# A state-space convolution with a gated FFN: tables loaded by pieces, negated sines made on chip, tensors given in the tiles' order, raw rows turned earlier

## The chip, the cores and the metric

The kernel runs on one core of a Trainium2 chip. The metric is the device time of one execution in microseconds (us), as a median over runs. The engines are TensorE (PE, matmuls), VectorE (DVE), ScalarE (ACT), GpSimd (POOL) and SyncE (SP, which here only issues DMAs). Each engine works through its own queue in order; engines wait for each other by semaphores. ACT and POOL can issue DMAs too.

## The reference

```python
x = A_u                                   # 1 x 2048 x 512
xn = layernorm(x)
K  = real(sum_n C[d,n] * exp(dt*A[d,n] * l) * dt*B[d,n])      # d: 512, l: 2048, n: 128
s  = irfft(rfft(xn, 4096) * rfft(K, 4096))[:2048] + xn * Dskip # causal convolution per channel
g  = silu(gelu(xn @ w1 + b1) @ w2 + b2)                        # 512 -> 1792 -> 512
return x + s * g
```

## The kernel before, in words

The first two thirds of the time go to the feed-forward part g (four tiles of 512 tokens, twice, once for each half of the hidden units) and, woven into it by the hand-written `ORDER` (L48), to the convolution kernel K. Both leave their results in DRAM: `gd` (the gate g, L186) and `kgd` (K, L190), and the normalized rows in `xs`. The time studied here is what follows.

**The seam** (L1037 to L1063). The last feed-forward pieces (`S`, `L`: `second_part`, dense matmuls of 128x512; `A`: silu on ACT) run between the first transforms of block 0 (`F00`, `F01`, `F10`, `F11`: `first_dft` on PE, L848, and `first_out`, L859, which copies its four PSUM banks to the tile X, two on ACT and two on DVE). Ahead of that loop stand, in the program: `z_load`, the load of the table `mc` in four pieces (`table_load`, L790), `side_skip(0)` on POOL (L843: adds the skip weight to block 0's kernel rows `in<-kgd`), `side_turn(1)` on ACT (L822: turns the 128x1024 halves of block 1's raw rows from `raw` into `in`), `kernel_load(1)` and `side_skip(1)`. Behind the loop come `z_store` (L438: the last tile of g goes to `gd`; four stores issued by POOL), then the loads of the tables `tcn` (four pieces) and `gc`. The tiles that the blocks use are opened over space that `zi`, the tile of g, has held.

**The blocks** (L1064). A Fourier transform of length 4096 is done as two transforms, 32 by 64. The 512 channels are four blocks of 128, each of eight slots (`slot(b, g)`, L966). A slot issues, in this order of the program:

- PE: the second transform `s` of four of the 32 frequencies (`second_dft`, L866, 64 matmuls of 64x64 against `mc`, which holds cosines, sines and negated sines); in some slots `sa`, the first inverse transform (`back_dft`, L904, against `tcn`); in slot 5 `y`, the last inverse transform of the block before (`last_dft`); in even slots the first transform of the next block.
- ACT: a copy `uh` of half of `s` (`spectrum`, L879), the copies Z out of `sa` (`back_out`, L914), the copies X out of the first transform.
- DVE: the products of both halves (`product`, L888), which free the PSUM tile of `s`, of which there are two; in slot 5 `last_out` (L954: four products of `y` with the gate `gb`, and on POOL four adds of x); in odd slots `combine` (L894: two adds into Y, which `sa` reads); the 32x32 transposes (`turn`).
- DMAs at the end of the slot: the gate and x for the block's output (`tail_load`, L932: in each of slots 0 to 3 two loads of `gb` and four of `xb`; x is read from the input in 512-byte rows), the raw rows two blocks ahead (`side_piece`, in slots 3 to 6), the output of the block before (`store`, L962, slot 7, 512-byte rows). In slot 7 ACT then turns the raw rows two blocks ahead (`side_turn`), both halves at once.

`bank` (L800) hands out the PSUM banks for the first transform, `sa` and `y` in turn, from two pools of two banks each; a first transform and a `y` take four, a `sa` two. A bank is free again when its copies or products have read it.

**The end** (L1067 to L1088). The last block's inverse transforms run split in halves: `sa` in two parts, transposes, `y` in two parts, then products and adds on DVE and POOL, and the store in eight DMAs, four on SP's queue and four on ACT's.

Of the kernel before, what the change touches and what calls it, by code (L numbers as in the profile page):

```python
# [11 lines left out]
F32 = mybir.dt.float32  # L12
# [8 lines left out]
P = 128  # L21
# [4 lines left out]
N1, N2 = 32, 64  # L26
NB = 4
# [103 lines left out]
def _shape_constants():  # L131
    n1 = np.arange(N1)[:, None]
    k1 = np.arange(N1)[None, :]
    a = 2 * np.pi * n1 * (k1 + 0.25) / N1
    cf = np.tile(np.stack([np.cos(a), -np.sin(a)], 1), (G, 1, 1))
    cg = np.stack([np.cos(a).T, -np.sin(a).T], 1).reshape(2, 2, 4, 2, 2, N1)
    cg = np.tile(cg.transpose(1, 3, 2, 4, 0, 5).reshape(1, N1, 2, N1), (G, 1, 1, 1))
    n2 = np.arange(N2)[:, None]
    k2 = np.arange(N2)[None, :]
    cm = np.zeros((2, N2, N1, 3, N2))  # L140
    ct = np.zeros((2, N2, N1, 2, N2))
    for k in range(N1):
        th = 2 * np.pi * (n2 * (k + 0.25) / L + n2 * k2 / N2)
        c, s = np.cos(th), np.sin(th)
        cm[:, :, k, 0, :] = c
        cm[:, :, k, 1, :] = s
        cm[:, :, k, 2, :] = -s
# [11 lines left out]
    return {  # L159
        "cf": cf.reshape(P, 2 * N1).astype(f),  # L160
        "cg": cg.reshape(P, 2 * N1).astype(f),
        "cm": cm.reshape(P, N1 * 3 * N2).astype(f),
        "ct": ct.reshape(P, N1 * P).astype(f),
        "cb": cb.reshape(CH * NPC, CH * NPH).astype(ml_dtypes.bfloat16),
    }
# [3 lines left out]
def kernel(  # L169
    ctx: ExitStack, tc: tile.TileContext,  # L170
    u, a_re, a_im, b_re, b_im, c_re, c_im, log_dt, dskip, w1, b1, w2, b2,
    cf, cg, cm, ct, cb, out,
# [3 lines left out]

    x_t = u[0].rearrange("(n w q) d -> w n q d", n=N1, w=4)
    o_t = out[0].rearrange("(n w q) d -> w n q d", n=N1, w=4)
    x_l = u[0].rearrange("(r j q) d -> j r q d", j=2, q=NQ)
# [3 lines left out]
    xs_l = xs.rearrange("(r j q) d -> j r q d", j=2, q=NQ)  # L183
    xt_h = [dram.tile([KD, P, TB * P], F32R, name=f"xt_h{t}") for t in range(NTB)]
# [124 lines left out]
    def ln_load(n):  # L309
        if n == 2:  # L310
            ln["zi"] = wka.tile([P, TB, D], F32, tag="zi", name="x23")
        if n in (2, 3):
            x = ln["zi"][:, 2 * n - 4:2 * n - 2, :]
        else:
            x = wka.tile([P, 2, D], F32, tag="x", name=f"x{n}", bufs=2)
        for j in range(2):
            SY.dma_start(x[j * 64:(j + 1) * 64], x_l[j, :, 2 * n:2 * n + 2, :])
        ln[n] = x
# [31 lines left out]
    def ln_store(n):  # L350
        for j in range(2):
            SY.dma_start(xs_l[j, :, 2 * n:2 * n + 2, :], ln[n][j * 64:(j + 1) * 64])

# [435 lines left out]

    def table_load(t, src):  # L790
        w = t.shape[2] if len(t.shape) == 3 else t.shape[2] * t.shape[3]
        for k in range(0, N1, 8):
            d = t[:, k:k + 8]
            SY.dma_start(d.rearrange("p k m -> p (k m)") if len(t.shape) == 3 else d.rearrange("p k a m -> p (k a m)"),
                         src[:, k * w:(k + 8) * w])

# [24 lines left out]

    def side_turn(b):  # L822
        if b:
            t = SB["pf"].tile([P, DB, N2], F32, tag="in", name=f"in0_{b}", bufs=2)
        else:
            t = wka.tile([P, DB, N2], F32, tag="xl", name="in0_0", bufs=2)
        raw = side[b].rearrange("p m d -> p d m")
        side[b] = [[t[:, :DB // 2], t[:, DB // 2:]]]
        for h in range(2):
            d, r = side[b][0][h], raw[:, h * DB // 2:(h + 1) * DB // 2]  # L830
            A.copy(d, r)

# [33 lines left out]
    def second_dft(b, g):  # L866
        mc = SB["mc"]
        p = SB["ps"].tile([P, 2, 2, 2, 2, N2], F32, tag="ri", name=f"s2_{b}_{g}", bufs=2)
        for jj in range(2):
            for o in range(2):  # L870
                for c in range(2):
                    for ka in range(2):
                        for r in range(2):
                            k, h = 4 * g + 2 * jj + ka, slice(r * 64, (r + 1) * 64)
                            PE.matmul(p[ka * 64:(ka + 1) * 64, r, o, :, jj], mc[h, k, ((0, 2), (1, 0))[c][o], :],  # L875
                                      xf[b][h, c, :, k, :], start=(c == 0), stop=(c == 1), skip_group_check=True)
        sp[b, g] = p
# [54 lines left out]
    def tail_load(b, t):  # L932
        if b not in gx:
            gx[b] = new_tail(b)
        gt, xt_ = gx[b]
        q = slice(t * TB, (t + 1) * TB)
        gv = gd[b][t].rearrange("(j n h) (q m) -> h j n q m", j=2, h=2, m=P)
        for h in range(2):
            SY.dma_start(gt[64 * h:64 * h + 64, q], gv[h])
            for w in (2 * h, 2 * h + 1):  # L940
                SY.dma_start(xt_[w * N1:(w + 1) * N1, q], x_t[w, :, q, b * P:(b + 1) * P])  # L941

# [11 lines left out]
    def last_out(b, py):  # L954
        gt, xt_ = gx[b]
        for g in range(G):
            cs = slice(g * N1, (g + 1) * N1)
            gv = gt[:, :, cs]
            V.tensor_mul(gv, py[g].rearrange("p (q i) -> p q i", i=N1), gv)
            GP.tensor_add(xt_[:, :, cs], gv, xt_[:, :, cs])  # L960

    def store(b, q=slice(0, NQ), qs=(SY, SY, SY, SY)):  # L962
        for w in range(4):
            qs[w].dma_start(o_t[w, :, q, b * P:(b + 1) * P], gx[b][1][w * N1:(w + 1) * N1, q])

    def slot(b, g):  # L966
# [49 lines left out]
        if last and 2 < g < 7:  # L1016
            tail_load(b, g - 3)
        if b + 2 < NB and 2 < g < 7:
            if g == 3:
                side[b + 2] = SB["pf"].tile([P, N2, DB], F32, tag="in", name=f"raw{b + 2}", bufs=2)  # L1020
            side_piece(b + 2, g - 3)
        if b and g == 7:
            store(b - 1)
        if b + 2 < NB and g == 7:
            side_turn(b + 2)
            kernel_load(b + 2)
# [66 lines left out]
_INS = ["A_u", "A_A_re", "A_A_im", "A_B_re", "A_B_im", "A_C_re", "A_C_im", "A_log_dt", "A_Dskip",  # L1093
        "B_w1", "B_b1", "B_w2", "B_b2"]
_OUTS = [((1, L, D), "float32")]

# [22 lines left out]
```

## Time and profile before

| | |
|---|---|
| runs shown | 574.71, 575.71, 577.72 us; median 575.71 |
| the profiled execution | 574.02 us |
| its span, first to last instruction | 572.2 us |
| mean granted TensorE clock | 0.974 |
| PE busy | 538.6 us, 94% of the span |
| DVE busy | 453.2 us, 79% |
| ACT busy | 402.8 us, 70% |
| POOL busy | 280.8 us, 49% |
| DMA | 86.92 MB, 109706 packets, 43606 of them under 512 B |

Lines of the timeline read: start in us, duration in us, engine, source line, operation, tile written <- tiles read, shapes, count of like instructions merged into the line; in brackets the idle time of the engine before it and what ended it. An engine's name with q (SPq) is its DMA issue. A line of the windows gives for a stretch, after its length, the busy time and count of PE, PE's weight loads, DVE, ACT and POOL, then the granted TensorE clock, the mean busy share of the 16 DMA engines, and GB/s.

### The profile page before, as it was taken

To read this page: it belongs to the slowest core of one execution; us is meant where nothing else is said; L and a number is where in the kernel's file an instruction comes from. 1 tells how busy PE (TensorE), PEld (TensorE's weight loads), DVE (VectorE), ACT (ScalarE), POOL (GpSimd) and SP (SyncE) were. 2 spreads that over 40 slices of the span, in tenths; PEclk is the share of its full clock that TensorE was granted. 3 is DMA by queue.
4 is the path that set the end of the run, shared out by engine and by line. 5 is a ranking of instruction groups with operands and counts; after the bars stand their busy time and mean duration, and the time that the engine had idled before them with its cause. 6 is when DMAs were issued, how large, how long until landed. Compare 5 with 4: busy or idle time off the path is not lost.

```text
span 572.2 us, 17585 instructions
## 1 busy us (share of the span) xinstructions
PE 538.6 (94%) x7471; PEld 429.7 (75%) x7471; DVE 453.2 (79%) x683; ACT 402.8 (70%) x578; POOL 280.8 (49%) x379
## 2 busy tenths in 40 slices
PE   8899999999999999999999999999969999999971
PEld 7667777777777777777777777777868898889760
DVE  6899989999899799997888867983433567777684
ACT  3588998889978989787997878896524744644320
POOL 5547388549876779968642963630100004012042
PEclk9999999999999999999999999999968999999985
DMA  8967545946391448470484149208926068734456
GB/s 193 276 187 222 164 130 159 253 124 203 82 343 37 126 158 239 148 194 21 111 245 124 38 104 162 48 21 265 409 88 76 18 178 133 179 98 106 133 146 137
DMA packets 109706, 86.92 MB, mean 152 GB/s; under 512 B 43606, under 2 KB 88922, under 8 KB 109628
## 3 DMA queue, kind: packets, MB, share of 16 engines
q1 hardware_dynamic: 99760, 67.45, 44.4%
q0 software_dynamic: 8768, 17.83, 10.3%
q8 instruction: 58, 0.95, 0.7%
q10 hardware_dynamic: 1100, 0.53, 0.4%
q14 instruction: 20, 0.16, 0.1%
HBM read 52.23 MB, written 33.55 MB: 150 GB/s over the span
## 4 chain that ended last, share of the span: by engine, by line
PE 61%; DVE 19%; SPq 5%; ACT 5%; DMA 4%; issue 4%; POOL 1%; DVEq 0%; ACTq 0%
PE s L875 8%; PE z L290 7%; PE z L291 6%; PE z L292 6%; PE f L251 6%; PE f L253 6%; PE f L252 6%; PE s L856 5%; PE kg L651 4%; SPq L941 4%; PE sa L911 3%; PE ph L590 2%; DVE hl L277 2%; DVE ra L604 2%; DMA out_dram<-xb 2%
## 5 line engine op out<-in xcount | busy, mean ns | idle before, releaser
L613 POOL TENSOR_TENSOR mm<-mm,rc 128x32 f32<-128x32 f32 (+4 forms) x150 | 116.3, 776 | 11.8
L290 PE MATMUL z<-w2h,hh 128*128 128x512 f32 x224 | 97.9, 437 | 0.0
L251 PE MATMUL f<-xh,w1h 128*128 128x512 f32 x220 | 91.3, 415 | 0.4 <-DVE xl L379 0.3
L292 PE MATMUL z<-w2h,hl 128*128 128x512 f32 x224 | 88.5, 395 | 0.3 <-DVE hl L277 0.3
L291 PE MATMUL z<-w2l,hh 128*128 128x512 f32 x224 | 88.6, 395 | 0.0
L253 PE MATMUL f<-xh,w1l 128*128 128x512 f32 x220 | 87.0, 395 | 1.5 <-DVE w1l L236 1.5
L252 PE MATMUL f<-xl,w1h 128*128 128x512 f32 x220 | 86.7, 394 | 0.0
L892 DVE TENSOR_TENSOR t<-s,uh 128x512 f32<-128x512 f32 x64 | 41.0, 682 | 44.9 <-ACT uh L883 35.1
L875 PE MATMUL s<-X,mc 64*64 64x128 f32 x2048 | 66.9, 281 | 5.7 <-issue 5.7
L875 PEld LDWEIGHTS s<-X,mc 64*64 64x64 f32 x2048 | 59.1, 138 | 11.7 <-issue 7.5
L277 DVE TENSOR_TENSOR hl<-hf,hh 128x512 fp32r<-128x512 f32 x56 | 51.3, 920 | 5.3 <-ACT hh L271 5.3
L610 POOL COPY mm<-rc 128x32 f32<-128x32 f32 x30 | 14.9, 497 | 77.5 <-DVE e L643 43.7
L604 DVE SCALAR_TENSOR_TENSOR ra<-ra,ph 128x512 f32<-128x512 f32 x64 | 43.6, 682 | 8.8 <-ACT ra L598 7.7
L253 PEld LDWEIGHTS f<-xh,w1l 128*128 128x128 f32 x220 | 41.3, 188 | 12.3 <-DVE w1l L236 2.4
L292 PEld LDWEIGHTS z<-w2h,hl 128*128 128x128 f32 x224 | 42.0, 188 | 11.1 <-DVE hl L277 1.2
L265 ACT ACTIVATE hf<-f,b1s 128x512 f32<-128x512 f32 x56 | 38.2, 687 | 17.1 <-DVE hl L277 6.0
L290 PEld LDWEIGHTS z<-w2h,hh 128*128 128x128 f32 x224 | 42.5, 190 | 9.9 <-ACT hh L271 0.4
L251 PEld LDWEIGHTS f<-xh,w1h 128*128 128x128 f32 x220 | 41.5, 189 | 10.0 <-issue 0.5
L291 PEld LDWEIGHTS z<-w2l,hh 128*128 128x128 f32 x224 | 42.3, 189 | 8.2 <-DVE w2l L236 0.2
L252 PEld LDWEIGHTS f<-xl,w1h 128*128 128x128 f32 x220 | 41.4, 188 | 9.1
L846 POOL TENSOR_TENSOR in<-in,dsk 128x16 f32<-128x16 f32 x8 | 1.8, 229 | 92.7 <-PE sa L911 57.7
L636 DVE TENSOR_TENSOR e<-mm,ra 128x1024 f32<-128x1024 f32 x32 | 42.5, 1327 | 5.5 <-POOL pr_h L519 2.9
(170 smaller groups left out, 1143.2 us busy)
## 6 DMA issues: line engine op xcount, KB each, us to landing
x<-in_A_u_dram SPq DMA_DIRECT2D x16, 256.0 KB
xs<-x SPq DMA_DIRECT2D x16, 256.0 KB
xt_h<-xh POOLq DMA_DIRECT2D x4, 1024.0 KB, 5.3
xt_l<-xl POOLq DMA_DIRECT2D x4, 1024.0 KB, 7.5
kgd<-ko SPq DMA_DIRECT2D x32, 128.0 KB
za<-zo SPq DMA_DIRECT2D x4, 1024.0 KB
xh<-xt_h POOLq DMA_DIRECT2D x4, 1024.0 KB, 6.1
xl<-xt_l POOLq DMA_DIRECT2D x4, 1024.0 KB, 10.4
```

Of the source, the lines that this page charges most:

```text
L251: PE.matmul(p, wh[:, k, :], xh[:, k, :], start=(k == 0), stop=False)
L252: PE.matmul(p, wh[:, k, :], xl[:, k, :], start=False, stop=False)
L253: PE.matmul(p, wl[:, k, :], xh[:, k, :], start=False, stop=(k == KD - 1))
L277: V.tensor_sub(hl, hf, hh)
L290: PE.matmul(z, hh[:, s], wh, start=(f0 == 0 and not rows), stop=False)
L291: PE.matmul(z, hh[:, s], wl, start=False, stop=False)
L292: PE.matmul(z, hl[:, s], wh, start=False, stop=(f0 == FA - 1))
L604: V.scalar_tensor_tensor(ra[:, 0, c], ra[:, 1, c], MAGIC, p, op0=ALU.subtract, op1=ALU.subtract)
L613: GP.tensor_mul(mv[:, :, 0:3:2, w:2 * w], mv[:, :, 0:3:2, 0:w], rc[:, 2 + 2 * i:4 + 2 * i, :].rearrange("p j c -> p c j").unsqueeze(3).to_ ...
L636: V.tensor_mul(e1, m1.unsqueeze(1).to_broadcast([P, 2, CH, N1]), ra[:, :, :, :N1])
L875: PE.matmul(p[ka * 64:(ka + 1) * 64, r, o, :, jj], mc[h, k, ((0, 2), (1, 0))[c][o], :], xf[b][h, c, :, k, :], start=(c == 0), stop=(c == 1 ...
L892: V.tensor_mul(t, p[:, i, :, 1].unsqueeze(1).to_broadcast([P, 2, 2, P]), uh)
```

## The change

- The host gives x a second time, as `ux`, already in the order of the tail's tiles, and the output is written in that order (the host puts it back). So `tail_load` makes two DMAs of 128 rows of 2 KB in place of six, `store` four such in place of four of 512-byte rows; the last store makes two on SP and two on ACT. The rows of x and `xs` are taken by 128-row tiles in another order of partitions, so that `gd` lies in the order of the tiles.
- `mc` has no negated sines. `mc_load(j)` loads a piece of 512 KB and has ACT write the negatives into `mn`. Pieces 0 and 1 come ahead of the loop of the seam, pieces 2 and 3 in block 0's slots 0 and 2. `ct_load(j)` loads `tcn` by pieces: piece 0 behind the loop, the others in slots 2, 4 and 6. Block 1's kernel rows are loaded in slot 1 of the program, and `side_skip(1)` is there too, behind `z_store` in POOL's queue.
- `side_turn(1)` is done by POOL. For blocks 2 and 3 the two halves are turned by ACT in slot 7 around `uh`, ahead of the copies Z, and the raw rows are loaded by slot 5.
- `last_out` comes behind `combine` in slot 5.
- Six small matmuls are put ahead of the last `y`.

In the built program PE, DVE and POOL keep their other instructions in the order of before. On ACT the two first `mn` stand between the last copy `ko` and the first copy X of block 0. On SP the two first pieces of `mc` are followed by piece 0 of `tcn`, `gc`, piece 2 of `mc`, block 1's kernel rows, piece 3 of `mc`, piece 1 of `tcn`, and then the raw rows of block 2.

```diff
-        SB["mc"] = pf.tile([P, N1, 3, N2], F32, name="mc")
+        SB["mc"] = pf.tile([P, N1, 2, N2], F32, name="mc")
+        SB["mn"] = pf.tile([P, N1, N2], F32, name="mn")
...
+    def mc_load(j):
+        k, w = slice(8 * j, 8 * j + 8), 16 * N2
+        SY.dma_start(SB["mc"][:, k].rearrange("p k a m -> p (k a m)"), cm[:, w * j:w * j + w])
+        A.mul(SB["mn"][:, k], SB["mc"][:, k, 1], -1.0)
+
+    def ct_load(j):
+        k, w = slice(8 * j, 8 * j + 8), 8 * P
+        SY.dma_start(SB["tcn"][:, k].rearrange("p k m -> p (k m)"), ct[:, w * j:w * j + w])
...
-    def side_turn(b):
...
+    def side_turn(b, hs=(0, 1), eng=A):
...
+        for h in hs:
+            d, r = side[b][0][h], raws[b][:, h * DB // 2:(h + 1) * DB // 2]
+            A.copy(d, r) if eng is A else eng.tensor_copy(d, r)
...
+                            w = mn[h, k] if o > c else mc[h, k, c != o]
...
+        for d, src in zip(gx[b], (gd[b][t], ux[b, t])):
+            SY.dma_start(d[:, t * TB:(t + 1) * TB].rearrange("p q m -> p (q m)"), src)
...
+    def store(b, t, q):
+        q.dma_start(out[b, t], gx[b][1][:, t * TB:(t + 1) * TB].rearrange("p q m -> p (q m)"))
...
+        turning = b + 2 < NB and g == 7
+        if turning:
+            side_turn(b + 2, (0,))
         spectrum(b, g)
+        if turning:
+            side_turn(b + 2, (1,))
         if sa:
             back_out(*sa)
...
         product(b, g)
-        if end:
-            last_out(b - 1, py)
...
             combine(b, i, 1)
             combine(b, i, 0)
+        if end:
+            last_out(b - 1, py)
...
+            for n in {3: (0,), 4: (1,), 5: (2, 3)}[g]:
+                side_piece(b + 2, n)
...
+        if b == 0 and g < 7:
+            if g in (0, 2):
+                mc_load(2 + g // 2)
+            if g == 1:
+                kernel_load(1)
+                side_skip(1)
+            if g in (2, 4, 6):
+                ct_load(g // 2)
...
         z_load(NTB - 1)
-        table_load(SB["mc"], cm)
+        for j in range(2):
+            mc_load(j)
         side_skip(0)
-        side_turn(1)
-        kernel_load(1)
-        side_skip(1)
+        side_turn(1, eng=GP)
...
-        table_load(SB["tcn"], ct)
+        ct_load(0)
...
+        idle = bank("idle")
+        for n in range(6):
+            PE.matmul(idle[:, 0], ident, ident, start=True, stop=True, skip_group_check=True)
...
-            store(b, q, (SY, A, SY, A))
+            for t in range(2 * s, 2 * s + 2):
+                store(b, t, (SY, A)[t % 2])
```

More of the change, by code (lines that the diff above doesn't have):

```diff
@@ L175 @@
     V, A, GP, PE, SY = nc.vector, nc.scalar, nc.gpsimd, nc.tensor, nc.sync
-    x_t = u[0].rearrange("(n w q) d -> w n q d", n=N1, w=4)
-    o_t = out[0].rearrange("(n w q) d -> w n q d", n=N1, w=4)
-    x_l = u[0].rearrange("(r j q) d -> j r q d", j=2, q=NQ)
+    x_l = u[0].rearrange("(n h j q) d -> h j n q d", n=N1, h=2, j=2)
     dram = ctx.enter_context(tc.tile_pool(name="dram", bufs=1, space=DRAM))
     xs = dram.tile([L, D], F32, name="xs")
-    xs_l = xs.rearrange("(r j q) d -> j r q d", j=2, q=NQ)
+    xs_l = xs.rearrange("(n h j q) d -> h j n q d", n=N1, h=2, j=2)
     xt_h = [dram.tile([KD, P, TB * P], F32R, name=f"xt_h{t}") for t in range(NTB)]
@@ L788, in open_mid @@
         SB["gc"] = pm.tile([P, 2, N1], F32, name="gc")
[L790 to L795, printed above, removed]
+    def mc_load(j):
[5 more added lines that the diff above has]
+        SY.dma_start(SB["tcn"][:, k].rearrange("p k m -> p (k m)"), ct[:, w * j:w * j + w])
     side, xf, fp = {}, {}, {}
@@ L820, in side_load @@
             side_piece(0, g)
-    def side_turn(b):
[L823 to L831, printed above, removed]
+    raws = {}
+    def side_turn(b, hs=(0, 1), eng=A):
+        if b not in raws:
+            if b:
+                t = SB["pf"].tile([P, DB, N2], F32, tag="in", name=f"in0_{b}", bufs=2)
+            else:
+                t = wka.tile([P, DB, N2], F32, tag="xl", name="in0_0", bufs=2)
+            raws[b] = side[b].rearrange("p m d -> p d m")
+            side[b] = [[t[:, :DB // 2], t[:, DB // 2:]]]
+        for h in hs:
+            d, r = side[b][0][h], raws[b][:, h * DB // 2:(h + 1) * DB // 2]
+            A.copy(d, r) if eng is A else eng.tensor_copy(d, r)
     def kernel_load(b):
@@ L874, in second_dft @@
                             k, h = 4 * g + 2 * jj + ka, slice(r * 64, (r + 1) * 64)
-                            PE.matmul(p[ka * 64:(ka + 1) * 64, r, o, :, jj], mc[h, k, ((0, 2), (1, 0))[c][o], :],
+                            w = mn[h, k] if o > c else mc[h, k, c != o]
+                            PE.matmul(p[ka * 64:(ka + 1) * 64, r, o, :, jj], w,
                                       xf[b][h, c, :, k, :], start=(c == 0), stop=(c == 1), skip_group_check=True)
@@ L1017, in slot @@
             tail_load(b, g - 3)
-        if b + 2 < NB and 2 < g < 7:
+        if b + 2 < NB and 2 < g < 6:
             if g == 3:
                 side[b + 2] = SB["pf"].tile([P, N2, DB], F32, tag="in", name=f"raw{b + 2}", bufs=2)
-            side_piece(b + 2, g - 3)
+            for n in {3: (0,), 4: (1,), 5: (2, 3)}[g]:
+                side_piece(b + 2, n)
         if b and g == 7:
-            store(b - 1)
+            for t in range(NTB):
+                store(b - 1, t, SY)
+        if b == 0 and g < 7:
[6 more added lines that the diff above has]
+                ct_load(g // 2)
         if b + 2 < NB and g == 7:
-            side_turn(b + 2)
             kernel_load(b + 2)
@@ L1117 @@
     r = _run(nc, [arrays], core_ids=[0])
-    return r.results[0]["out_0_dram"]
+    o = r.results[0]["out_0_dram"].reshape(NB, NTB, 4, N1, TB, P)
+    return o.transpose(3, 2, 1, 4, 0, 5).reshape(1, L, D)
```

29 lines of the change are left out of this document (10 added, 19 removed).

## The prediction

> **What bounds the kernel now.** I read the page first, then the windows and the timeline around the seam between the feed-forward part and the convolution blocks, then the timeline at the block seams and at the end.
>
> ```profile
> span 572.2 us, 17585 instructions
> ...
> PEclk9999999999999999999999999999968999999985
> ```
>
> This row is the clock that TensorE (PE) was granted, in 40 slices of 14.3 us. It dips twice, in slices 30 and 31 (415 to 443 us) and in the last two. Where it is full PE is nearly always busy, as in the first line of the windows below (2.00 of 2.00 us), and its work stays the same, 64 matmuls for 64; what the change can win lies in the dips and at the seams of the blocks.
>
> ```profile
> 402.00:404.00 2.00, 2.00 (x55) 1.64 (x57) 0.88 (x2) 0.00 (x0) 0.00 (x0) 1.00 1.02 414
> ...
> 416.00:418.00 2.00, 0.32 (x8) 0.08 (x1) 0.00 (x0) 0.50 (x2) 0.00 (x0) 1.00 0.96 305
> 418.00:420.00 2.00, 0.44 (x6) 0.20 (x5) 0.00 (x0) 0.58 (x1) 0.00 (x0) 0.91 0.27 98
> ...
> 432.00:434.00 2.00, 2.00 (x30) 1.80 (x24) 1.00 (x2) 0.58 (x1) 0.00 (x0) 0.68 1.44 163
> ```
>
> Around 416 to 420 PE almost stops, the granted clock falls to 0.50, and it comes back only between 432 and 434. The timeline tells how the seam is built.
>
> ```profile
> 392.84 3.93 ACT L831 COPY in<-raw 128x1024 f32<-128x1024 f32 x2
> ...
> 394.38 1.95 SPq L794 DMA_DIRECT2D mc<-in_cm_dram  x4
> ...
> 397.59 1.07 ACT L862 COPY X<-s 128x512 f32<-128x512 f32 x2 [0.82 <-ACT in L831]
> ...
> 398.23 2.75 PE L856 MATMUL s<-fc,in 32*128 32x64 f32 x64 [0.60 <-ACT X L862]
> ...
> 401.01 0.23 POOL L846 TENSOR_TENSOR in<-in,dsk 128x16 f32<-128x16 f32 x1 [1.01 <-DMA in<-kgd]
> ```
>
> In the first fence line ScalarE (ACT) turns the raw rows of block 1 (L831), so its first X copy starts at 397.59 and PE's second first-transform (L856) waits for that copy. The first half of block 0's kernel rows (`in<-kgd`) has landed before 401; the second half at 401.0, when GpSimd (POOL) gets its add. The four pieces of `mc`, 768 KB each, stand behind them in the same queue, and the windows show that this queue moves 414 GB/s.
>
> ```profile
> 409.48 1.96 PE L875 MATMUL s<-X,mc 64*64 64x128 f32 x58
> ...
> 409.79 1.23 ACT L432 ACTIVATE zi<-zi 128x512 f32<-128x512 f32 x2 [0.40 <-DVE zi L429]
> ...
> 411.41 0.23 POOL L846 TENSOR_TENSOR in<-in,dsk 128x16 f32<-128x16 f32 x1 [10.17 <-DMA in<-kgd]
> ...
> 412.83 2.98 POOL L441 DMA_DIRECT2D gd<-zi  x4
> ...
> 420.55 1.89 DVE L892 TENSOR_TENSOR t<-s,uh 128x512 f32<-128x512 f32 x3 [6.64 <-DMA gd<-zi]
> ...
> 421.34 3.69 PE L875 MATMUL s<-X,mc 64*64 64x128 f32 x64 [2.66 <-issue]
> ...
> 432.20 2.56 PE L911 MATMUL sa<-tcn,Y 64*128 64x128 f32 x32
> ```
>
> At 409.48 PE starts block 0. The last silu ends at 411.02, but `z_store` stands in POOL's queue behind `side_skip(1)`, which waits for block 1's kernel rows, themselves behind 3 MB of `mc`. So the stores issue at 412.83, VectorE (DVE) may write its second product (its buffer lies where `zi` was) only at 420.55, and the third s matmul group starts at 421.34, at half clock: 3.69 us.
>
> ```profile
> 392.97 1.91 DMA kgd<-ko
> ...
> 434.76 1.91 PE s L875 x64
> ```
>
> At full clock such a group takes 1.91.
>
> **Part by part.** *The negated sines* (L774 to L795). Each `mn` piece is an ACT activation of 128x512; its price is that of silu's.
>
> ```profile
> L432 ACT ACTIVATE zi<-zi x4: 630/631/647, 406.9 to 410.4; 128x512 f32<-128x512 f32 x4
> ```
>
> Four cost 2.5 us on ACT. Two of them sit late, in slots 0 and 2, behind X copies that have left, with nothing due soon behind them: 0. The remaining table pieces are issued by SP ahead of their slots (`tcn` 2 and 3 between the raw rows, which wait for slot 2's first transform; they are due in slot 7 and in block 1's slot 1): 0, unless that transform slips by more than four slots. The other two stand in ACT's queue ahead of the first X copies and wait for `mc` pieces 0 and 1. Behind them on ACT wait the X copies, and for these PE's F01 matmuls. The pieces are 0.524 MB now; at 414 GB/s each takes 1.27 us after the 401.0 landing, so 402.3 and 403.5 (the bound below is 401.0, if they travel beside the kernel rows and not behind them). The second `mn` ends at 404.2, where before the X copies began at 397.59: **+6.6 us** for PE, which has nothing else that may pass. That the two raw turns leave ACT wins nothing against this.
>
> PE then stands for some 7 us from 397.6, longer than the 5 us that dropped the clock in the windows above, so it resumes at half clock. How long? In the windows it stayed low for 12 us of s and first-transform matmuls on parts of the array; here dense 128x512 feed-forward matmuls follow F01. Bounds: nothing, and 12 us cold, a loss of 0 to 6; I take 6 us, F01 at half clock (3.7) and the dense matmuls behind it, **+3.0**. [...] ACT's and DVE's copies don't slow with PE, and the 0.75 us by which F01 was stretched (2.75 against 2.0 for 64) goes partly: **-0.5**. Block 0 starts at 409.5 + 9.1 = 418.6, silu ends at 420.1.
>
> *What that buys.* By then all tables have landed: 2 MB of `mc`, 1 MB of `tcn`, 1 MB of kernel rows at 414 GB/s need some 10 us from 401. `side_skip(1)` now stands behind `z_store`, so the stores issue at once, the last at 422.4.
>
> ```profile
> DMA to landing us min/median/max: 5.5/5.5/5.6
> ```
>
> Before, a store landed 5.5 us after its issue, with the queue full; the small `kgd` store took 1.91 alone. I take 3.5 (both ends kept): 425.9, product to 426.6, third s group at 426.7. PE idles about 2 us for it, from 424.5, too short to lose the clock. Before, the group began at 421.3, but cold: sa(0,0) ended at 434.76 by the row of 432.20. Warm, the s and first-transform groups between and sa take some 1.95 each, four of them, so sa ends at 434.5. **The seam as a whole: -0.2.** The loss at 398 is about paid back at 416 to 433.
>
> *Block 1's raw rows turned on POOL* (`side_turn(1, eng=GP)`). No row shows this copy: 128x1024 read with a stride.
>
> ```profile
> L615 POOL TENSOR_TENSOR mm<-mm,rc 128x512 f32<-128x512 f32 x30 | 38.6, 1287 | 2.4
> ...
> L610 POOL COPY mm<-rc 128x32 f32<-128x32 f32 x30 | 14.9, 497 | 77.5 <-DVE e L643 43.7 <-DMA rc<-recd 33.8
> ```
>
> By elements of the large add, twice 1287 = 2.6 us; by the small copy's 15.5 ns an element, 16. I take the first, since the small one is nearly all fixed cost. Two end at 406, hidden under PE until 420; the cover ends at 9.5 us each, as `z_store` is behind them. [...]
>
> *Raw rows turned early in slot 7* (blocks 0 and 1).
>
> ```profile
> 447.10 2.05 ACT L862 COPY X<-s 128x512 f32<-128x512 f32 x4 [1.26 <-PE s L856]
> ...
> 449.10 0.58 ACT L883 COPY uh<-s 128x512 f32<-128x512 f32 x1
> ...
> 451.00 1.07 ACT L922 COPY Z<-sa 128x512 f32<-128x512 f32 x2 [1.32 <-PE sa L911]
> 451.04 0.69 DVE L902 TENSOR_TENSOR Y<-t,t 128x512 f32<-128x512 f32 x1
> ...
> 451.96 3.88 ACT L831 COPY in<-raw 128x1024 f32<-128x1024 f32 x2
> ...
> 454.02 2.01 PE L856 MATMUL s<-fc,in 32*128 32x64 f32 x64 [1.15 <-ACT in L831]
> ```
>
> Now PE's L856 waits 1.15 us for the turn. After, ACT runs from 449.15: first half 1.94, uh 0.58, second half 1.94, then the two Z copies, ending 454.15 and 454.7. The first half is no longer late. But L856 takes four banks, two of them the sa banks that the Z copies free, so Z is late next: its full stretch starts near 454.7 instead of 454.05: **+0.6, twice: +1.2** (from -1.1, if Z did not hold it, to +0.8 each).
>
> *Combine ahead of the tail products at g = 5.*
>
> ```profile
> 476.40 2.48 DVE L959 TENSOR_TENSOR gb<-y,gb 128x512 f32<-128x512 f32 x4 [0.24 <-PE y L952]
> ...
> 478.29 2.06 PE L911 MATMUL sa<-tcn,Y 64*128 64x128 f32 x32
> ```
>
> In blocks 1 and 2 the four gb products start 1.4 us later (two adds of 0.69 as in the fence above), and the second frees its bank at 478.8 instead of 477.6; sa wants it at 478.3: **+0.5, twice: +1.0** (0 to 1.0). In block 3 it is the other way.
>
> ```profile
> 543.53 2.48 DVE L959 TENSOR_TENSOR gb<-y,gb 128x512 f32<-128x512 f32 x4 [3.47 <-PE y L952]
> ...
> 547.29 1.74 DVE L900 TENSOR_TENSOR Y<-t,t 128x512 f32<-128x512 f32 x1
> ...
> 549.17 4.58 PE L911 MATMUL sa<-tcn,Y 64*128 64x128 f32 x48 [2.03 <-DVE Y L900]
> ...
> 558.81 0.73 PE L952 MATMUL y<-T,gc 32*32 32x256 f32 x32 [1.96 <-DVE T L928]
> ...
> 559.94 1.17 PE L952 MATMUL y<-T,gc 32*32 32x256 f32 x32 [0.40 <-DVE T L928]
> ```
>
> There DVE idles until 543.53, then runs the products, then two Y adds until 549.03, and sa waits 2.03 us for Y. With Y ahead of them, in the idle time, the rest of DVE's chain (products, adds, transposes, which set the end) moves up by the 3.0 that Y took behind the products, less what POOL's adds, beside which Y's second add took 1.74 and not 0.69, now slow the next ones: **-2.2** (0 to -3.0). The six idle matmuls cover the wait for the transposes; the last y group, 1.17 at half clock, goes to the 0.73 of the group before: **-0.4**.
>
> *Loads and stores in the tiles' order.* Fewer issues on SP; no wait of PE in the fences ends on one of these loads, so within the blocks 0.
>
> ```profile
> 543.13 0.45 SPq L939 DMA_DIRECT2D last<-gd  x1
> ...
> 565.01 3.12 SPq L964 DMA_DIRECT2D out_dram<-last  x4
> ```
>
> The final store was four issues on each of SP and ACT, 3.12 us, of 512-byte rows. Two issues of 0.45 remain on each, the last by 566.0 instead of 568.1. The data moved at
>
> ```profile
> 566.00:570.00 4.00, 0.00 (x0) 0.00 (x0) 0.00 (x0) 0.00 (x0) 0.00 (x0) 0.50 1.01 227
> ```
>
> 227 GB/s. Bounds: 0, if the data and not the issues set the end (1.05 MB in 4.6 us either way), and -3.1, the issues' 2.1 and 1.0 for the last half MB at 414. I take **-2.6**, nearer the issues, which ran to 4 us before the end of the span.
>
> x loads and stores of the prologue keep 4 KB rows: 0.
>
> **Sum:** -0.2 + 1.2 + 1.0 - 2.2 - 0.4 - 2.6 = -3.2 us. The profiled execution took 574.02 (572.2 and 1.8 around it), so 570.8; it lies 1.7 under the median of the runs, 575.71, from which I forecast **572.5**.
>
> **Rivals.** *A, the wait is short.* If the `mc` pieces share the engines with the kernel rows, the X copies start near 401; the idle time is too short for a cold clock, silu ends near 414 and the third s group starts warm near 420: the seam gives -7, in all 565.7. Against it: the kernel halves landed 1.2 us apart, in order. *B, the clock stays low* as long as in the trace, 12 us: +3, no gain left, 575.5. For it: that is the one long case shown. *C, a second fall.* If `z_store` lands in 5.5 us instead of 3.5, PE idles over 4 us ahead of the third s group. Should that suffice to drop the clock (it decides at some 3.5 us; between 416 and 421 it took two gaps with 6 matmuls between), partial-array matmuls run cold for 12 us: +2 + 6 on the sum: 580.5, slower. Against it: no other traffic then. *D, POOL's copies take 16 us each:* `z_store` slips from 420 to 433, +13: 585.5. That the wait on ACT is not there at all gives A's time too.
>
> **Numbers.** Forecast 0.48 (own range 570 to 575), A 0.12, B 0.18, C 0.17, D 0.05. Range 567.5 to 580.5: it leaves out D and the low part of A, and some of C. A measurement can tell about 0.5% (2.9 us) from no change: of the forecast's 0.48, 0.31 are faster by more. Faster 0.31 + 0.12 = 0.43, same 0.17 + 0.18 = 0.35, slower 0.22.
>
> **What would show it.** ACT: two `mn` before the first X copy, the second ending near 404; PE idle 397.6 to 404.8; granted clock 0.50 for some 6 us then and 1.00 from 416 on; POOL's `gd<-zi` straight behind the last silu; L856 at the block seam waiting for Z instead of `in`; sa in block 3 waiting for nothing; one store issue of some 0.45 for each of the four final pieces. It is wrong if the first X copy starts before 401, if the clock stays low past 412, or if POOL's copies reach past 415.

## The result, and the profile after

The changed kernel takes 699.03 us (median of 4 runs, 693.39 to 702.66) against 575.21 us for the kernel before (4 runs): a ratio of 1.2135, 95% interval 1.2038 to 1.2231. The forecast was 572.5 us with a range up to 580.5. The profiled execution took 701.03 us, its span 699.3. Runs over 1.5% slower than the fastest of the same kernel are left out of what follows: one of e1 (589.44 us) and two of e4 (575.18 and 575.87), with which the medians are the 583.36 and 569.13 us that some expectations quote.

The page of the changed kernel: the span, PE's busy share in 40 slices (17.5 us each), the granted clock, and the busy share of the DMA engines.

```profile
span 699.3 us, 17526 instructions
...
PE   5233329956596959999999999999959799999983
...
PEclk9565659978798989999999999999966799999997
DMA  1312134515252428444851391292381445460722
```

The dip of the clock at the seam is still there (slices 30 to 32). But the loss lies where neither the prediction nor any of its rivals looked: in slices 2 to 6 PE is busy for two to three tenths of the time only, the clock is low there too, and the DMA row begins with 1, 3, 1, 2. The windows of the prologue, first after and then before (columns as explained ahead of the change; the last two are the mean busy share of the 16 DMA engines and GB/s):

```profile
8.00:10.00 2.00, 2.00 (x20) 2.00 (x19) 0.00 (x0) 0.45 (x1) 1.40 (x8) 1.00 0.13 51
```

```profile
8.00:10.00 2.00, 2.00 (x21) 2.00 (x20) 1.86 (x6) 0.84 (x2) 1.40 (x8) 1.00 1.23 167
```

In the changed kernel the DMA engines carry 51 GB/s at a share of 0.13, that is 2 of 16, where the kernel before moves 167 GB/s at a share of 1.23, so with all of them. The queue of SP, after and then before, shows what is carried so slowly:

```profile
0.74 4.98 SPq L314 DMA_DIRECT2D x<-in_A_u_dram  x4
...
41.22 15.61 SPq L349 DMA_DIRECT2D xs<-x  x4
...
102.96 0.33 SPq L547 DMA_DIRECT2D pcd<-pc  x1
```

```profile
0.75 2.50 SPq L317 DMA_DIRECT2D x<-in_A_u_dram  x4
...
15.11 3.18 SPq L352 DMA_DIRECT2D xs<-x  x4
...
34.46 0.33 SPq L550 DMA_DIRECT2D pcd<-pc  x1
```

The first four issues take 4.98 us instead of 2.50, the first four stores `xs<-x` 15.61 instead of 3.18, and everything that follows in this one queue is late with them: the first `pcd` store, whose data the kernel K needs, issues at 102.96 instead of 34.46. The view of the tile x says who waited, for how many us in all and how often, first after and then before:

```profile
  DVE bst L319: 54.7, 6
```

```profile
  DVE bst L322: 4.1, 1
```

VectorE's statistics of the rows wait 54.7 us for these loads, and waited 4.1. ScalarE waits 71.2 us for weights (`w1s`) that stand behind them in the same queue. The loss grows to 113 us by the start of the seam, where PE's first transform of block 0 begins, after and then before:

```profile
503.97 0.43 PE L859 MATMUL s<-fc,in 32*128 32x64 f32 x2
```

```profile
391.04 0.43 PE L856 MATMUL s<-fc,in 32*128 32x64 f32 x2
```

Behind it the seam adds 11 us (to the end of the first `sa`: 558.99 and 434.76) and the rest of the kernel 3. The seam after:

```profile
515.32 0.63 ACT L791 ACTIVATE mn<-mc 128x512 f32<-128x512 f32 x1 [9.45 <-DMA mc<-in_cm_dram]
...
517.85 4.17 PE L859 MATMUL s<-fc,in 32*128 32x64 f32 x64 [7.30 <-ACT X L865]
...
536.49 0.94 PE L879 MATMUL s<-X,mc 64*64 64x128 f32 x16
...
545.60 1.89 DVE L896 TENSOR_TENSOR t<-s,uh 128x512 f32<-128x512 f32 x3 [5.42 <-DMA gd<-zi]
...
546.39 0.67 PE L879 MATMUL s<-X,mc 64*64 64x128 f32 x16 [3.80 <-issue]
...
556.39 2.60 PE L915 MATMUL sa<-tcn,Y 64*128 64x128 f32 x32
```

ScalarE's two negations wait 9.45 us for the tables, the first X copy starts at 517.23, PE stands for 7.30 us, and later another 3.80 us for VectorE's product (545.60), which waits for the gate's stores. The clock in two stretches of it:

```profile
512.00:514.00 2.00, 0.00 (x0) 0.00 (x0) 0.00 (x0) 0.00 (x0) 0.23 (x1) 0.80 1.02 401
...
536.00:538.00 2.00, 2.00 (x46) 1.51 (x48) 0.70 (x2) 1.26 (x2) 0.00 (x0) 0.72 0.00 0
```

It falls at 513 and is back at 537; the rows of 546 (0.84) and 556 (0.60) put a second fall at 547 and its end at 557.6.

### The profile page after: what moved, and what is told of

Read it like the earlier page. It is cut to its first block, busy times and chain, and to the rows that moved or that the text cites. A ratio compares the mean times of both kernels' runs of the same rounds, so it can differ in the third digit from the quotient of the medians.

```text
span 699.3 us, 17526 instructions
## 1 busy us (share of the span) xinstructions
PE 565.2 (81%) x7483; PEld 451.5 (65%) x7483; DVE 447.0 (64%) x683; ACT 403.0 (58%) x580; POOL 280.1 (40%) x381
## 4 chain that ended last, share of the span: by engine, by line
PE 57%; DMA 16%; DVE 10%; SPq 10%; issue 3%; ACT 2%; DVEq 0%; ACTq 0%
PE s L879 9%; PE z L287 6%; PE z L288 5%; PE z L289 5%; PE s L859 5%; PE f L248 5%; PE f L250 5%; PE f L249 5%; DMA x<-in_A_u_dram 5%; PE sa L915 4%; PE kg L648 3%; DMA xs<-x 3%; DMA w1s<-in_B_w_dram 3%; SPq L349 3%; SPq L214 3%
## 5 line engine op out<-in xcount | busy, mean ns | idle before, releaser
L248 PE MATMUL f<-xh,w1h 128*128 128x512 f32 x220 | 94.5, 430 | 30.9 <-ACT w1h L231 30.9
L289 PE MATMUL z<-w2h,hl 128*128 128x512 f32 x224 | 92.1, 411 | 14.7 <-DVE hl L274 14.7
L287 PE MATMUL z<-w2h,hh 128*128 128x512 f32 x224 | 102.5, 458 | 0.0
L288 PE MATMUL z<-w2l,hh 128*128 128x512 f32 x224 | 92.0, 411 | 0.0
L587 PE MATMUL ph<-cbs,lh 96*128 96x512 bf16 x64 | 26.0, 406 | 37.3 <-DMA lh<-pcd 30.6
L879 PEld LDWEIGHTS s<-X,mc 64*64 64x64 f32 x1536 | 48.5, 142 | 9.4 <-issue 5.5
L287 PEld LDWEIGHTS z<-w2h,hh 128*128 128x128 f32 x224 | 44.9, 200 | 12.7 <-issue 2.5
L288 PEld LDWEIGHTS z<-w2l,hh 128*128 128x128 f32 x224 | 44.7, 199 | 9.0 <-DVE w2l L233 0.2
L859 PE MATMUL s<-fc,in 32*128 32x64 f32 x1024 | 42.8, 310 | 9.2 <-ACT X L865 7.3
L274 DVE TENSOR_TENSOR hl<-hf,hh 128x512 fp32r<-128x512 f32 x56 | 46.3, 831 | 5.3 <-ACT hh L268 5.3
```

The lines of the kernel that those rows point to most:

```text
L248: PE.matmul(p, wh[:, k, :], xh[:, k, :], start=(k == 0), stop=False)
L274: V.tensor_sub(hl, hf, hh)
L287: PE.matmul(z, hh[:, s], wh, start=(f0 == 0 and not rows), stop=False)
L288: PE.matmul(z, hh[:, s], wl, start=False, stop=False)
L289: PE.matmul(z, hl[:, s], wh, start=False, stop=(f0 == FA - 1))
L859: PE.matmul(p[:, i, :], src[r, 2 * i:2 * i + 2, :], fc[r], start=True, stop=True, skip_group_check=True)
```

## The experiments

Theory 1: the new views of x and `xs`, `(n h j q) d -> h j n q d`, make each transfer of 64 rows one of 2 x 32 rows, and with this 2 as its slowest dimension only 2 of the 16 DMA engines carry it (the share of 0.13 above). Its edit in the change, which the section on the change gives in words only:

```diff
-    x_l = u[0].rearrange("(r j q) d -> j r q d", j=2, q=NQ)
+    x_l = u[0].rearrange("(n h j q) d -> h j n q d", n=N1, h=2, j=2)
...
-            SY.dma_start(x[j * 64:(j + 1) * 64], x_l[j, :, 2 * n:2 * n + 2, :])
+            SY.dma_start(x[j * 64:(j + 1) * 64], x_l[j, :, :, 2 * n:2 * n + 2, :])
```

and the same for the store. Rivals: the addresses of the new row order are slow; a view of four dimensions is slow in itself; the number of issues costs; another part of the change does it.

### e1: rows by 32

```diff
-        for j in range(2):
-            SY.dma_start(x[j * 64:(j + 1) * 64], x_l[j, :, :, 2 * n:2 * n + 2, :])
+        for w in range(4):
+            SY.dma_start(x[w * 32:(w + 1) * 32], x_l[w // 2, w % 2, :, 2 * n:2 * n + 2, :])
```

(the store likewise)

> The changed kernel with each x load and each xs store of 64 rows made as two of 32 rows (one for each value of j): the same rows at the same addresses, twice as many issues, and the slowest dimension of a transfer is 32 and no longer 2. Theory 1 (two of the 16 DMA engines carried each of these transfers, since their slowest dimension was 2): the first 10 us move some 170 GB/s or more instead of 33, the first pcd store is issued near 35 us instead of 103, the first transform of block 0 starts near 391 instead of 504, so 113 us go: 699 - 113 = 586 us. What is left over the kernel before is the seam and the blocks, +11. Rival 2 (the order of the rows is slow by itself: the addresses step by 32 and 128 KB): nothing changes, near 699. Rival 3 (the number of DMA issues on SP is the cost): it gets slower still, over 700. My prediction, had only its term for the x rows been wrong: 572.5.

Measured: 580.72 us (578.50 to 586.00, 3 runs) against 573.16: 1.0147, 1.0073 to 1.0222. The same rows at the same addresses, with twice the issues, and 118.3 us are gone. That rules out the addresses and the number of issues. A window of the prologue, and the start of block 0's first transform:

```profile
7.00:9.00 2.00, 2.00 (x20) 2.00 (x19) 1.85 (x4) 0.47 (x1) 1.57 (x6) 1.00 1.08 186
```

```profile
390.34 0.43 PE L859 MATMUL s<-fc,in 32*128 32x64 f32 x2
```

The share is back above 1; the first transform of block 0 begins at 390.34. What is left of the seam in this run comes below.

### e2: the kernel before with the new rows

```diff
-    x_l = u[0].rearrange("(r j q) d -> j r q d", j=2, q=NQ)
+    x_l = u[0].rearrange("(n h j q) d -> h j n q d", n=N1, h=2, j=2)
...
-        gv = gd[b][t].rearrange("(j n h) (q m) -> h j n q m", j=2, h=2, m=P)
+        gv = gd[b][t].rearrange("(h r) (q m) -> h r q m", h=2, m=P)
```

> The kernel before with nothing but the new order of the x rows (views of x and xs in four dimensions, and the gate's load in the tail in the order that follows from it). Theory 1: 575 + 113 = 688 us, DMA share near 0.13 in the first 10 us. If the other parts of the change were to blame: near 575. Rival 2 (addresses): 688 as well; the run with rows by 32 tells these two apart.

Measured: 683.3 us, one run, and in its prologue the row

```profile
5.00:9.00 4.00, 4.00 (x31) 4.00 (x31) 0.00 (x0) 0.62 (x1) 2.81 (x15) 1.00 0.13 49
```

By this run the rows alone cost the kernel before 110 us. No other part of the change is needed for the loss.

### e3: the loads only

As e1, but with the edit for the load alone.

> The changed kernel with only the x loads made of 32 rows each; the xs stores keep the slowest dimension of 2. Theory 1: the stores still take two engines for 5 us each and still block what is queued behind them on those two engines; by count half of the 32 transfers are mended, so some half of the 113 us goes: 640 us, between 610 and 670. If only the loads matter, because the first tiles wait for them: near 586. If only the stores matter: near 699.

Measured: 636.84 us, one run. Stores on two engines cost 56 us of the 118, by the difference from e1: about half, as by the count.

### e5: one load of 128 rows

```diff
-    x_l = u[0].rearrange("(n h j q) d -> h j n q d", n=N1, h=2, j=2)
+    x_w = u[0].rearrange("(n w q) d -> w n q d", n=N1, w=4)
...
-        for j in range(2):
-            SY.dma_start(x[j * 64:(j + 1) * 64], x_l[j, :, :, 2 * n:2 * n + 2, :])
+        SY.dma_start(x, x_w[:, :, 2 * n:2 * n + 2, :])
```

(the store likewise)

> The changed kernel with the two x loads of a tile made as one of 128 rows, and the two xs stores as one: same rows, same addresses, same form in four dimensions, but the slowest dimension is 4 (the four values of h and j) and not 2. Theory 1 (as many engines carry a transfer as divide its slowest dimension, here 4): the mean busy share of the 16 DMA engines in the first 10 us is near 0.25 instead of 0.13, a transfer has twice the bytes and the same time, so half of the 113 us goes: 642 us, between 625 and 660. Rival (a view of four dimensions is slow in itself, whatever its sizes): near 699. Rival (the number of issues): halved too, but then the run with twice as many issues of 32 rows would have been slower and not 116 us faster.

Measured: 620.5 us, one run; of the 118 us a third is left and not half, so the size was missed by 21 us and lies below the expected 625 to 660. The mechanism was not missed: a window of the prologue shows

```profile
13.00:15.00 2.00, 0.00 (x0) 0.00 (x0) 1.57 (x4) 0.00 (x0) 0.00 (x0) 0.68 0.26 106
```

a share of 0.26, 4 of 16, and 106 GB/s, twice the changed kernel's. The view has four dimensions here too, so these are not slow in themselves: with a 4 in front in place of the 2 it moves twice as much. Per engine it is the same each time: 51 GB/s over 2 engines, 106 over 4 and, from the window rows in the prediction, 414 over 16 are 25.5, 26.5 and 25.9. The first statistics start at 15.5 us after the start of the changed kernel, at 12.2 here and at 5.1 in e1; probably more of the transfers hide beside other work behind the first tiles, so that half the time per byte costs less than half, but no run here shows that.

So the shares of 0.13, 0.26 and, in the window of e1, 1.08 go with a slowest dimension of 2, 4 and 32. These are the only sizes that the experiments show; that the engines have to divide the size, as the expectation has it, was the author's theory and is not shown.

### e4: the negatives later

On top of e1, `mc_load` only loads, and ScalarE's negation of a piece is a step of its own, `mn_make`, issued later for the first two pieces:

```diff
                 first_out(0, *k, (A, A, V, V))
+                if k[0]:
+                    mn_make(k[1])
```

> As the run with rows by 32, and besides ScalarE makes the first two pieces of negated sines behind the X copies of F10 and F11 and not ahead of the first X copy. Theory (the wait of the two pieces for the mc tables stops PE at the seam, about 8 us, and the clock then stays at half for some 20 us): PE does not stop at the second first transform, the clock stays full until block 0, so block 0 starts 14 us earlier than in the run with rows by 32: 586 - 14 = 572 us; the third s group still waits for the gd stores. Rival (the tables' traffic or another wait holds the seam anyway): within 3 us of the run with rows by 32. If the clock falls all the same at the wait for the gd stores, some 3 us more than 572.

Measured: 568.87 us (566.34 to 572.39, 8 runs) against 573.16: 0.993, 0.9897 to 0.9962. The seam of e1, then of e4:

```profile
403.16 0.63 ACT L791 ACTIVATE mn<-mc 128x512 f32<-128x512 f32 x1 [0.65 <-DMA mc<-in_cm_dram]
...
404.32 4.17 PE L859 MATMUL s<-fc,in 32*128 32x64 f32 x64 [7.40 <-ACT X L865]
...
418.77 0.67 PE L879 MATMUL s<-X,mc 64*64 64x128 f32 x16
...
427.89 1.89 DVE L896 TENSOR_TENSOR t<-s,uh 128x512 f32<-128x512 f32 x3 [5.71 <-DMA gd<-zi]
...
428.68 0.67 PE L879 MATMUL s<-X,mc 64*64 64x128 f32 x16 [4.08 <-issue]
```

```profile
393.01 0.43 PE L862 MATMUL s<-fc,in 32*128 32x64 f32 x2
...
400.11 2.66 PE L862 MATMUL s<-fc,in 32*128 32x64 f32 x64 [0.52 <-ACT X L868]
...
411.27 0.67 PE L882 MATMUL s<-X,mc 64*64 64x128 f32 x16
...
419.57 1.89 DVE L899 TENSOR_TENSOR t<-s,uh 128x512 f32<-128x512 f32 x3 [4.43 <-DMA gd<-zi]
...
420.36 0.67 PE L882 MATMUL s<-X,mc 64*64 64x128 f32 x16 [2.47 <-issue]
```

In e1 PE waits 7.40 us for the X copy behind the negations; in e4 0.52. From the first transform to block 0's first s group it is 28.4 us in e1 (390.34 to 418.77), 18.3 in e4 and 18.4 in the kernel before (391.04 to 409.48). The clock stayed at 1.00 in all of e4's seam, also behind the 2.47 us ahead of the third s group.

### e6: the gate stored by pieces

On top of e4, each piece of the last gate tile is stored behind its silu:

```diff
-    gd = [dram.tile([NTB, P, TB * P], F32, name=f"gd{b}") for b in range(NB)]
+    gda = dram.tile([NB, NTB, P, TB * P], F32, name="gda")
+    gd = [gda[b] for b in range(NB)]
...
+    def piece_store(t, i):
+        d = gda[:, t].rearrange("b p (q m) -> p b q m", m=P)[:, :, i]
+        (A if i == TB - 1 else GP).dma_start(d, fin[t][:, i, :].rearrange("p (b m) -> p b m", m=P))
...
                 silu(NTB - 1, int(p[1]))
+                piece_store(NTB - 1, int(p[1]))
...
-        z_store(NTB - 1)
```

> As the run with the negatives made later (569.13 us), and besides the last tile of the gate goes to DRAM by its four pieces, each as soon as its silu is done (three issued by GpSimd, the last by ScalarE), and not in four stores behind the last silu. Theory (the third s group waits for VectorE's product, that for the landing of the stores, 4.43 us of idle time there and 2.47 on PE): the last store is issued near 413.5 instead of 415.4 and lands near 417, so the third s group starts by 418 instead of 420.4: 2 to 2.5 us less, 566.7. Rival (the stores land no earlier, since the tables' loads keep the DMA engines busy until then): the same as 569.1.

Measured: 566.89 us (566.62 to 568.60, 4 runs) against 574.18: 0.9865, 0.9814 to 0.9916. The last store now issues at 411.76, and the product follows at 417.70:

```profile
411.76 0.41 ACTq L443 DMA_DIRECT2D gda<-zi  x1
...
417.70 0.69 DVE L904 TENSOR_TENSOR t<-s,uh 128x512 f32<-128x512 f32 x1 [3.53 <-DMA gda<-zi]
417.71 0.27 PE L887 MATMUL s<-X,mn 64*64 64x128 f32 x1 [1.30 <-issue]
...
418.50 0.67 PE L887 MATMUL s<-X,mc 64*64 64x128 f32 x16 [0.20 <-issue]
```

The third s group starts at 418.50, 8.4 us behind block 0 (410.10); in e4 it was 9.1. What is left is mostly another wait: 1.30 us in which PE waited for nothing that the profile shows.

### e9: the pieces alone

On top of e1, the edit of e6 without that of e4.

> The run with rows by 32 (583.36 us median, the negatives ahead of the first X copy), with only the gate stored by its pieces. This is the seam as my prediction had it: one stop for the tables near 398 to 404, and stores that land soon enough for the third s group. Theory (two stops at the seam, each followed by a fall of the clock: 7.4 us idle and three windows of half clock, then 4.1 us idle and one window): the second stop shrinks below 2 us and no fall follows it, 4 to 5 us less: 578.5. Rival (only the first stop matters, the second is hidden by what it delays): within 1.5 us of 583. What the stop for the tables costs by itself is then the distance to the run with both mended (566.89): about 12 us.

Measured: 576.52 us (572.87 to 580.27, 10 runs) against 574.15: 1.0027, 0.9986 to 1.0068; it was expected at 578.5. (What the expectation counts as three windows of half clock and one are e1's low stretches of 10.2 and 3.4 us.) So the stop for the tables costs 9.6 us by itself (576.52 less 566.89), the stop for the stores 4.2 behind the other (580.72 less 576.52), and 2.0 alone (568.87 less 566.89). The last two are rough: the runs of e1 and e4 scatter over 7.5 and 6 us.

### e7: the turn late again

As e4, with `side_turn` back at the end of slot 7.

> As the run with the negatives made later, but the raw rows of blocks 2 and 3 are turned as in the kernel before, both halves behind uh and the copies Z at the end of slot 7. My prediction had priced the early turn at +0.6 us at each of two block seams; in the profiles the distance from sa in slot 7 to the first transform of slot 0 was 5.10 and 5.11 us before and is 5.04 and 4.87 us in the run with the negatives made later. If those rows are right, the distances go back to 5.1 and the time is the same within 0.5 us (569 us); if the prediction's term was right, 1.2 us less.

Measured: 574.22 us, one run. The distances from `sa` to the first transform go back to 5.11 and 5.10 us, as expected; in e4 they are 5.04 and 4.87. But they end where the transform, in e4 its longer part, begins, and so leave out what comes of it. The first of each, on to the next `sa`, e7 and then e4:

```profile
448.06 2.06 PE L918 MATMUL sa<-tcn,Y 64*128 64x128 f32 x32
...
453.17 2.01 PE L862 MATMUL s<-fc,in 32*128 32x64 f32 x64 [1.16 <-ACT in L837]
...
457.02 2.06 PE L918 MATMUL sa<-tcn,Y 64*128 64x128 f32 x32
```

```profile
441.75 2.06 PE L918 MATMUL sa<-tcn,Y 64*128 64x128 f32 x32
...
446.79 2.56 PE L862 MATMUL s<-fc,in 32*128 32x64 f32 x60 [0.70 <-ACT Z L929]
...
452.71 2.06 PE L918 MATMUL sa<-tcn,Y 64*128 64x128 f32 x32
```

From `sa` to the next `sa` it is 8.96 us in e7 and 10.96 in e4, and 8.95 and 9.19 at the second seam; the kernel before has 8.96 at both. So the early turn costs 2.0 and 0.2 us there: 60 matmuls take 2.56 us where 64 took 2.01, and at the first seam the clock falls in e4 for 3.4 us besides, worth up to 1.7:

```profile
450.00:452.00 2.00, 2.00 (x44) 2.00 (x41) 0.47 (x1) 1.15 (x3) 0.46 (x2) 0.50 1.03 369
```

The total went up by 5 and not by 0.3, for another reason: after the wait for the gate's stores the clock fell in this run (0.50 from 422 to 432) and in e4's profile it did not, though PE had stood 2.49 us here and 2.47 there.

```profile
422.00:424.00 2.00, 2.00 (x40) 1.67 (x36) 1.14 (x3) 0.59 (x1) 0.00 (x0) 0.50 0.00 0
```

### e8: the products first

As e4, with `last_out` ahead of `combine` in blocks 1 and 2.

> As the run with the negatives made later, but in slot 5 of blocks 1 and 2 the products of the tail stand ahead of combine again, as in the kernel before; block 3 keeps the new order. The prediction priced the new order at +0.5 us in each of the two blocks; in the profiles the way from y to the sa of slot 7 was 11.27 and 11.23 us before and is 11.48 and 11.51 us now. Expected: 11.25 each, so 0.5 us less in all, not to be seen in the total (568.6 us) but in these rows.

Measured: 566.44 us, one run. In e8, `y` and the `sa` of slot 7 of block 1:

```profile
467.24 2.35 PE L954 MATMUL y<-T,gc 32*32 32x512 f32 x64
...
478.47 2.06 PE L918 MATMUL sa<-tcn,Y 64*128 64x128 f32 x32
```

That is 11.23 us, against 11.48 in e4 (469.38 to 480.86); in block 2 it is 11.23 against 11.51. The new order costs 0.25 and 0.28.

### e10: all that helps

e6 with the edit of e8.

> Rows by 32, the negatives later, the gate by pieces, and in slot 5 of blocks 1 and 2 the products ahead of combine: every part of the change that the rows showed to help, in the place where it helps. From the run with the gate by pieces (566.89) less the 0.5 us of the two slots: 566.4 us, between 564 and 568, against 574 before: a ratio near 0.986. If the two slots' gain is hidden, 566.9.

Measured: 567.35 us (565.72 to 568.25, 6 runs) against 574.15: 0.9875, 0.9828 to 0.9921. This version beats both kernels, by about 7 us (1.25%) and 132 us; the half microsecond of e8 isn't seen in the total.

## Why the prediction was wrong, point by point

**The step that failed** is the last of the part on loads and stores: "x loads and stores of the prologue keep 4 KB rows: 0." The rows are 4 KB, and that was taken for the whole price. What changed is the shape in front of the rows, 2 x 32 where 64 stood, and with it the number of engines: e1 and e2 put this step at +118 and +110 us. That a 2 in front leaves 2 engines, only the runs show (a share of 0.13 in the changed kernel and in e2), no row of the kernel before. With it, and 26 GB/s for each engine (414 over 16), the size can be estimated: 256 KB on 2 engines take 5.0 us, and there are 32 such transfers in the one queue that feeds the prologue, up to 161 us. The prediction also looked for the change's effects only behind 390 us, where the table of dips had drawn the eye, and left the part of the kernel where PE was busy without a second look at the DMAs that keep it busy.

The other steps, read in e1, where this one is mended, or in the run that is named (e1's first transform of block 0 starts 0.70 us earlier than that of the kernel before, which is allowed for):

- *The negations stop PE* (+6.6): right. The second `mn` ends at 403.79 (forecast 404.2), and the first X copy is at 403.70, 6.8 us later than before. The wait is real, and e4 takes it away.
- *The clock after it* (+3.0, for 6 us of half clock): the mechanism right, the size not settled. The low stretch lasted from 402 to 412 in e1's profile and from 513 to 537 in the changed kernel's, where 6 us were forecast. From the first transform to block 0 it is 10.0 us more than before in e1, near the forecast 9.1, and 14.1 in the changed kernel.
- *What that buys* (back to -0.2): wrong, by a mis-sized term. The third s group was forecast at 426.7, warm; it came at 428.68, and the clock fell again. The landing was taken as 3.5 us:

```profile
DMA to landing us min/median/max: 2.8/4.2/5.4
```

the median is 4.2 in e1 (3.5 in the changed kernel), but the product waits for the last of four, 5.4 us. This is rival C, with its mechanism (PE idle for 4.08 us, a second fall at 429.4) and a chance of 0.17. That its time of 580.5 us is nearly e1's 580.72 is luck: C had the second low stretch at 12 us and it lasted 3.4, and over the kernel before C had 4.8 us and e1 has 7.6. `sa` ends at 438.10: the seam costs +4.0 in e1 and +11.3 in the changed kernel.
- *POOL's copies* (2.6 us each): 1.92 each; hidden, as forecast.
- *The early turn* (+1.2): right in sign and mechanism, too small. Z is the last to come, as forecast (0.70 us, in the fence of e4); from `sa` to the next `sa` the two seams cost 2.0 and 0.2 us in e4, by e7, and up to 1.7 of it is a fall of the clock that the forecast did not have.
- *Combine before the products* (+1.0): right in sign, +0.5 by e8. In block 3, with the idle matmuls (-2.2 and -0.4): from the start of `y` to the end of the last `y` it was 21.14 us before (539.97 to 561.11) and is 19.45 after, 670.40 to 689.85, so -1.7. The end of the changed kernel:

```profile
677.51 2.06 PE L915 MATMUL sa<-tcn,Y 64*128 64x128 f32 x32
...
680.35 1.16 PE L915 MATMUL sa<-tcn,Y 64*128 64x128 f32 x16 [0.78 <-DVE Y L904]
...
682.63 2.31 PE L951 MATMUL y<-T,gc 32*32 32x512 f32 x32 [1.12 <-DVE T L932]
...
693.75 0.88 SPq L962 DMA_DIRECT2D out_dram<-last  x2
```

`sa` starts without a wait, as forecast, where before it waited 2.03 us as a whole; its second part now waits 0.78, and a new wait of 1.12 for the transposes gives part of it back. The last `y` group takes 0.73 (from 689.12), as forecast.
- *The final store* (-2.6): two issues of 0.44 on each queue, as forecast, but from the first issue to the end of the span 5.55 us, and 7.19 before: -1.6. That the data sets the rest is likely, but not shown.

Behind the seam the forecast had -3.0 us in all (+1.2, +1.0, -2.2, -0.4 and -2.6), and no profile shows a gain there. From the end of the first `sa` to the end of the span it is 137.44 us before, 138.36 in e9 and 140.31 in the changed kernel. The end of the kernel, from the start of `y` in block 3's slot 5 (539.97 before, 547.96 in e9, 670.40 in the changed kernel), gains 3.7 and 3.3 us where 5.2 were forecast; the blocks ahead of it lose 4.6 and 6.2 where 2.2 were. In these blocks the clock falls for 3.4 us once in e9, at 458.9, and twice in the changed kernel, at 581.5 and 612.2, and not in the profile of the kernel before. At up to 1.7 us each, this is the largest part that was found. Its cause stays open: e7, with the turn late again, has such a fall too, at 483.3.

e9, with the rows mended and the stores landing soon, is the kernel that the forecast of 572.5 describes. It takes 576.52, which lies in the range, but it is no faster than the kernel before. The span of its profiled execution is 4.3 us longer than before (576.5 and 572.2), where the forecast had it 3.2 shorter. Of these 7.5 us 3.6 lie in the seam, where the low clock lasted 23.9 us and not 6, and 3.9 behind it.

## What to carry to other kernels

Ahead of any estimate of a DMA, read the sizes of its view from the slowest dimension inwards, and compare them with those before: here a new order of rows that put a 2 in front left 14 of 16 engines idle (a share of 0.13, 51 GB/s), at the same bytes and the same row length. A wait for several transfers is as long as the slowest of them, not as their median (5.4 and 4.2 us in e1). What a shift of work costs is read from one event to the same event of the next slot, not to the first instruction that moved. And a negation, a cast or a turn that waits for a load belongs behind the work that its engine has ready, since all of that stands in line after it (PE waited 7.40 us behind the negations in e1, 0.52 in e4).

## What of the hardware was not expected

In these profiles the low clock comes in whole steps. Worked out from the granted clock of the window rows (0.91 from 418 to 420 is a fall at 419.6), it lasted 10.2 us in e1 (402.2 to 412.4), 13.6 in the kernel before (419.6 to 433.3), and 23.9 both in the changed kernel and in e9: 3, 4, 7 and 7 times 3.41 us (23.9 over 7). PE's program at this place is the same in e1, e9 and the changed kernel. In e9:

```profile
406.00:408.00 2.00, 2.00 (x48) 2.00 (x44) 0.00 (x0) 0.00 (x0) 0.00 (x0) 0.50 1.02 410
...
424.00:426.00 2.00, 2.00 (x61) 1.83 (x57) 0.30 (x1) 0.63 (x1) 1.15 (x3) 0.81 0.77 229
```

PE was busy all the time from 406 to 424 us and the clock was still 0.50; it rose within the last of these rows. So 18 us of busy PE did not lift it there, while in e1 it was back 8.1 us after PE had resumed (404.3 to 412.4). Nor is an idle stretch of some length a sure cause. From PE's stop to the fall it was 3.3 us in the kernel before (416.3 to 419.6, six matmuls between), 3.5 in e9 (397.3 to 400.9), 5.2 in e1 (396.9 to 402.2) and 2.6 in the changed kernel (510.6 to 513.2). A whole stop of 2.49 us sufficed in e7, and one of 2.03 in the kernel before (547.1 to 549.2, the fall at 549.4); 2.47 in e4 and 2.52 in e8 did not. So neither the forecast's 2 us, "too short to lose the clock", nor rival C's "some 3.5 us" is a bound that holds for all of them. And in the changed kernel the clock fell at 612.2 us though PE had been busy for at least 1.84 of each 2 us from 592 on:

```profile
612.00:614.00 2.00, 2.00 (x52) 2.00 (x48) 0.00 (x0) 2.00 (x5) 0.00 (x0) 0.55 0.81 297
```

What lets the clock fall and what brings it back stays open. Between e1 and e9 the length of the low clock is worth up to 6.9 us at this seam (half of 23.9 less 10.2), and the runs of one kernel differ with it (the kernel before, beside e9: 570.40 us at a mean clock of 0.982, 577.90 at 0.963).
